# The order of two DFTs turned round, with block products in the second

## The chip, the cores and the metric

The kernel runs on one core of one Trainium2 chip. The metric is the device time of one execution in microseconds. A core has a matrix engine (TensorE, PE in the profile, with its weight loads as PEld), three elementwise engines (VectorE or DVE, ScalarE or ACT, GpSimd or POOL), and SyncE (SP), which here issues the DMAs. Each engine works through its own list of instructions in order; a DMA issued by SP or POOL waits in that list until its buffers are free.

## The reference

```python
x = A_x                                             # 2048 tokens x 448
n = layernorm(x)
a = n @ dft_hid_re.T ; b = n @ dft_hid_im.T         # DFT over the 448 features
h = x + dft_seq_re @ a - dft_seq_im @ b             # DFT over the 2048 tokens, real part
m = layernorm(h)
out = h + (gelu(m @ w_gate) * (m @ w_up)) @ w_down  # 448 -> 1792 -> 448
```
All inputs are float32.

## The kernel before

Every float32 operand of a matmul is kept as two float16 parts, a high half written by ACT (`hi_part`, line 105) and a low half written by DVE (`lo_part`, lines 109 and 111), and a product is three matmuls: high by high, low by high, high by low.

**The DFT stage.** The sequence DFT runs first, on the normalised x. There are four blocks b of 512 output tokens and 16 chunks c of 128 input tokens, so 64 steps n. In a step, `seq_mm` (line 412) holds a 128 x 128 piece of x as the stationary operand and streams 512 columns of W past it; the last 64 features of both parts (re and im) share one bank and are done by `seq_mm_rest` (line 426), two matmuls side by side in the array. Seven PSUM banks collect a block. W arrives as 128 x 1024 float32 tiles (`seq_load`, five buffers), and `seq_hi` and `seq_lo` split it three steps ahead. When a block is done, `z_out` moves the banks to SBUF in two halves, and `hid_mm` (line 477) does the feature DFT: 21 matmuls of 448 columns for each 128 tokens, whose result DVE adds to x (line 485). These follow some steps into the next block, from the table `after`.

Beside this, written out by step number in `early` and `after`: the 14 tiles of gate/up weights (`Weights`: load, sums on DVE, split, store to DRAM), the second layernorm and its operands for the first two quarters of tokens (`ffn_stats` to `ffn_transpose`), the store of h, and the first loads and sums of w_down. PE starts with 56 transposes that have no use but activity (line 99).

**The feed-forward stage.** `GateUp` makes products of blocks (line 716, 256 columns) for 4 quarters of tokens x 14 tiles of features, steps t = 0 to 55. From t = 14, `dn_mm` multiplies by w_down with seven block products in place of eight (line 660, 224 columns). `down_prep(t)` prepares w_down in steps 0 to 14: POOL makes sums of blocks, ACT and DVE split them into `wd`. `gw_load` fetches the stored weight tiles again, two steps ahead, into three buffers.

Of the kernel before, what the change touches and what calls it, by code (L numbers as in the profile page):

```python
# [11 lines left out]
ALU = mybir.AluOpType  # L12
# [20 lines left out]
def kernel(  # L33
# [55 lines left out]
    sign_t = const.tile([P, 1], F32, name="sign_t")  # L89
    G.memset(sign_t[:64], D_SC)  # L90
    G.memset(sign_t[64:], -D_SC)

# [4 lines left out]
    pw = ps_tr.tile([P, 8, P], F16, tag="tr", name="pw")  # L97
    for k in range(56):
        PE.transpose(pw[:, k % 8, :], ident, ident)  # L99
# [61 lines left out]
    def pair_tile(name):  # L161
        return ring.tile([P, 2, D], F32, tag="xh", bufs=5, name=name)

    def w_tile(name):
        return ring.tile([P, 28 * P], F16, tag="w", bufs=3, name=name)
# [125 lines left out]


    class Weights:


        def __init__(self, f):
            self.f = f
            self.raw = dft.tile([P, 2, 6, P], F32, tag="raw", bufs=2, name=f"gu_raw{f}")
            for r in range(2):
                nc.sync.dma_start(self.raw[:, r], w_gu[f, :, r])  # L300

        def sums(self):
            gate, up = self.raw[:, 0], self.raw[:, 1]
            s = self.s = dft.tile([P, 10, P], F32, tag="s", name=f"gu_s{self.f}")
            V.tensor_add(s[:, 0:3], up[:, 0:3], up[:, 3:6])
            V.tensor_sub(s[:, 3:6], s[:, 0:3], gate[:, 0:3])
            V.tensor_sub(s[:, 6:8], gate[:, 0:2], up[:, 0:2])
            V.tensor_sub(s[:, 8:10], gate[:, 4:6], s[:, 4:6])
# [15 lines left out]
        def split(self, of_raw):  # L324
            if of_raw:
                self.w = w_tile(f"gu_w{self.f}")
# [9 lines left out]
    xt, xs, norm_x = {}, {}, {}  # L336

    def x_load(i):
        xt[i] = dft.tile([P, 1, D], F32, tag="xt", bufs=3, name=f"x{i}")
        nc.sync.dma_start(xt[i][:, 0, :], x[i * P : (i + 1) * P, :])  # L340

    def x_stats(i):
        mv = stats(xt[i], f"x{i}")
        norm_x[i] = mv, root(mv, f"x{i}")

    def x_norm(i):
        mv, sd = norm_x.pop(i)
        xn = xt[i][:, 0, :]
        normed(xn, xn, mv, rstd(mv, sd, f"x{i}"), 0)
        xs[i] = dft.tile([P, 2, D], F16, name=f"xs{i}")  # L350
        hi_part(xs[i][:, 0], xn)

    def x_lo(i):
        lo_part(xs[i][:, 1], xt[i][:, 0, :], xs[i][:, 0])

    wr, ws = {}, {}

    def seq_load(n):
        wr[n] = dft.tile([P, 8 * P], F32, tag="wr", bufs=5, name=f"wr{n}")
        b, q, jj = n // NT, n // 2 % 8, n % 2
        nc.sync.dma_start(wr[n], w_seq[(2 * b + jj) * 8 + q])

    def seq_hi(n):
        if n % 2 == 0:
            ws[n // 2] = dft.tile([P, 2, 2, 8 * P], F16, tag="ws", bufs=4, name=f"ws{n // 2}")
        hi_part(ws[n // 2][:, 0, n % 2], wr[n], D_SC)

    def seq_lo(n):
        t = ws[n // 2][:, :, n % 2]
        lo_part(t[:, 1], wr[n], t[:, 0], D_SC)


    def first_load(c, jj):
        if c == 0:
            wr[jj] = dft.tile([P, 8 * P], F32, tag="wr", bufs=5, name=f"wr{jj}")
        if c == jj == 0:
            ws[0] = dft.tile([P, 2, 2, 8 * P], F16, tag="ws", bufs=4, name="ws0")  # L380
        cols = slice(c * P, (c + 1) * P)
        nc.sync.dma_start(wr[jj].rearrange("p (b t) -> p b t", b=4)[:, :, cols], w_seq[jj * 8][:, :, cols])

    def first_views(c, jj):
        cols = slice(c * P, (c + 1) * P)
        ts = [wr[jj], ws[0][:, 0, jj], ws[0][:, 1, jj]]
        return [t.rearrange("p (b t) -> p b t", b=4)[:, :, cols] for t in ts]

    def first_hi(c, jj):
        src, hi, lo = first_views(c, jj)  # L390
        hi_part(hi, src, D_SC)

    def first_lo(c, jj):
        src, hi, lo = first_views(c, jj)
        lo_part(lo, src, hi, D_SC)

    def seq_w(n, l, part):

        t = ws[n // 2][:, l].rearrange("p a (r g c t) -> p r c a g t", r=2, g=2, c=2)
        return t[:, part, n % 2]  # L400

    TERMS = ((0, 0), (1, 0), (0, 1))
    acc = {}

    def seq_mm(n, parts, terms=range(3)):

        b, c = divmod(n, NT)
        for part in parts:
            for k in range(3):
                for m in terms:  # L410
                    lx, lw = TERMS[m]
                    PE.matmul(  # L412
                        acc[b, 3 * part + k],
                        xs[c][:, lx, k * P : (k + 1) * P],
                        seq_w(n, lw, part),
                        start=c == 0 and m == 0,
                        stop=c == NT - 1 and m == 2,
                    )

    def seq_mm_rest(ns):  # L420

        for n in ns:
            b, c = divmod(n, NT)
            for m, (lx, lw) in enumerate(TERMS):
                for part in range(2):
                    PE.matmul(  # L426
                        acc[b, 6][64 * part : 64 * part + 64, :],
                        xs[c][:, lx, 3 * P :],
                        seq_w(n, lw, part),
                        start=c == 0 and m == 0,  # L430
                        stop=c == NT - 1 and m == 2,
                        skip_group_check=True,
                    )

    z = {}

    def z_out(b, k):
        if k == 0:
            z[b] = dft.tile([P, 2, 7, TB], F16, tag="z", name=f"z{b}")
        sc = 1.0 / (X_SC * D_SC)  # L440
        ps = acc.pop((b, k))
        hi_part(z[b][:, 0, k], ps, sc)
        lo_part(z[b][:, 1, k], ps, z[b][:, 0, k], sc)


    wh = dft.tile([P, 2, 7, D], F16, name="wh")
    wh_raw = {}

    def wh_load(g):

        t = wh_raw[g] = dft.tile([P, (3, 3, 1)[g], D], F32, tag="raw", bufs=2, name=f"wh_raw{g}")
        if g < 2:
            nc.sync.dma_start(t, w_hid[:, 0:3, g * D : (g + 1) * D])
        else:
            for r in range(2):
                nc.sync.dma_start(t[64 * r : 64 * r + 64, 0], w_hid[64 * r : 64 * r + 64, 3, r * D : (r + 1) * D])

    def wh_split(g):
        src = wh_raw[g]
        k = slice(3 * g, 3 * g + src.shape[1])  # L460
        sc = (D_SC, -D_SC, sign_t)[g]
        hi_part(wh[:, 0, k], src, sc)
        lo_part(wh[:, 1, k], src, wh[:, 0, k], sc)

    hp = {}
    xr = x.rearrange("(k g j p) d -> k j p g d", k=2, g=2, j=4)

    def h_tile(q, j):
        hp[q, j] = pair_tile(f"hx{q}_{j}")
        nc.sync.dma_start(hp[q, j], xr[q // 2, 2 * (q % 2) + j])  # L470

    def hid_mm(b, i, pool, tag):

        y = pool.tile([P, 512], F32, tag=tag, name=f"y_{b}_{i}")
        for k in range(7):
            for m, (lz, lw) in enumerate(((0, 0), (0, 1), (1, 0))):
                PE.matmul(  # L477
                    y[:, :D],
                    z[b][:, lz, k, i * P : (i + 1) * P],
                    wh[:, lw, k, :],  # L480
                    start=k == 0 and m == 0,
                    stop=k == 6 and m == 2,
                )
        h = hp[b, i // 2][:, i % 2, :]
        V.scalar_tensor_tensor(h, y[:, :D], 1.0 / D_SC, h, op0=ALU.mult, op1=ALU.add)  # L485

    def h_store(q, j):
        nc.sync.dma_start(h_dram[2 * q + j], hp[q, j])


    N_STEPS = NB * NT
    gu = {}

    early, after = {}, {}

    def at(where, n, *what):
        where.setdefault(n, []).extend(what)

    for g in range(3):
        at(early, 5 + 2 * g, lambda g=g: wh_load(g))  # L500
        at(early, 7 + 2 * g, lambda g=g: wh_split(g))

    for k, f in enumerate(reversed(range(NF))):
        n = 17 + 3 * k
        at(early, n - 4, lambda f=f: gu.update({f: Weights(f)}))
        at(early, n, lambda f=f: gu[f].sums())
        at(early, n + 1, lambda f=f: gu[f].split(True))
        at(early, n + 2, lambda f=f: gu[f].split(False), lambda f=f: gu[f].store())
    for b in range(NB):
        for j in range(2):  # L510
            n = (b + 1) * NT + 1 + 6 * j
            at(early, min(n - 4, N_STEPS - 3), lambda b=b, j=j: h_tile(b, j))
            if b == NB - 1:
                continue
# [15 lines left out]
    for c in range(2):  # L530
        for jj in range(2):
            first_load(c, jj)
# [608 lines left out]
```

## Time and profile before

| what | value |
|---|---|
| median of 3 runs | 732.07 us (731.82 to 732.6) |
| profiled execution: first to last instruction | 730.1 us |
| around that span, against the median of the runs | 2.0 us |
| PE busy | 718.5 us (98%) |
| DVE / ACT / POOL busy | 523.0 / 277.9 / 242.1 us |
| moved by DMA | 139.84 MB, mean 192 GB/s |

The profiled execution has no time of its own apart from its span; the 2.0 us are the distance to the median of the other runs. In the profile, a group of instructions is given as line, engine, operation, output<-inputs, shapes and count, then the busy time, the mean time of one in ns, and the idle time of the engine just before them with what ended it. Matmuls overlap in the array, so their pace is read from the chain of work, where one piece begins when the piece before lets it.

### The profile page before, as it was taken

The page shows a single profiled execution, that of the slowest core. Times are in us where ns is not written, and L with a number is a line of the kernel's source. Part 1 is how long each engine was busy: PE and PEld are TensorE (multiplying, and loading weights), DVE is VectorE, ACT ScalarE, POOL GpSimd, SP SyncE. Part 2 cuts the span into 40 slices and gives each one's busy share as a digit, 9 for nine tenths or more (in the row PEclk, how much of TensorE's full clock was granted, in tenths as well). Part 3 has the DMA queues.
Part 4 walks back from the last instruction along what each step waited for, and adds up shares of the span by engine and source line. Part 5 has one row for each costly group of instructions (what it writes and reads, how often), then busy time and mean ns, then how long its engine had stood idle before and what let it go on. Part 6 is the DMA issues. An engine that isn't in the chain of part 4 may idle for free.

```text
span 730.1 us, 13452 instructions
## 1 busy us (share of the span) xinstructions
PE 718.5 (98%) x5309; PEld 497.9 (68%) x5309; DVE 523.0 (72%) x1071; ACT 277.9 (38%) x544; POOL 242.1 (33%) x281
## 2 busy tenths in 40 slices
PE   9999999999999999999999999999999999999987
PEld 5444444444444444444588889999999999999977
DVE  7888667486665866441377778787887877989794
ACT  4444703256233442311043444442444434454421
POOL 0000000000000001000057865576685867768360
PEclk9999999999999999999999999999999999999999
DMA  8667466577667976530057654747447676555311
GB/s 280 227 218 235 163 231 208 185 211 256 231 214 218 316 253 241 219 122 5 26 206 262 240 207 167 181 168 209 176 147 225 186 213 228 219 179 185 127 39 39
DMA packets 63503, 139.84 MB, mean 192 GB/s; under 512 B 30288, under 2 KB 39504, under 8 KB 63440
## 3 DMA queue, kind: packets, MB, share of 16 engines
q1 hardware_dynamic: 63440, 138.99, 57.2%
q8 instruction: 41, 0.67, 0.4%
q14 instruction: 22, 0.18, 0.1%
HBM read 112.23 MB, written 20.19 MB: 181 GB/s over the span
## 4 chain that ended last, share of the span: by engine, by line
PE 93%; DVE 4%; DMA 1%; ACT 1%; issue 1%; POOL 0%; POOLq 0%; DVEq 0%; ACTq 0%
PE acc L412 34%; PE pY L716 13%; PE acc_d L660 12%; PE y L477 9%; PE pZ L716 9%; PE pX L716 9%; PE acc L426 6%; DMA gw<-w_dram 1%; PE pw L99 1%; DVE last_v L900 1%; DVE last_a L109 1%; DVE last_s L904 1%; PE last_Y L879 1%; PE last_X L879 1%; DVE last_s L903 0%
## 5 line engine op out<-in xcount | busy, mean ns | idle before, releaser
L412 PE MATMUL acc<-ws,xs 128*128 128x512 f16 x1152 | 253.8, 379 | 0.0
L716 PEld LDWEIGHTS <-gw 128*128 128x128 f16 x2067 | 201.9, 98 | 24.1 <-issue 2.4
L412 PEld LDWEIGHTS <-xs 128*128 128x128 f16 x1152 | 111.3, 98 | 138.3 <-issue 6.5
L716 PE MATMUL pY<-hops,gw 128*128 128x256 f16 x901 | 123.0, 273 | 1.9 <-DVE u L726 1.7
L660 PE MATMUL acc_d<-wd,dn_w 128*128 128x224 f16 x882 | 105.1, 259 | 0.0
L203 POOL TENSOR_TENSOR wd_s<-wd 128x448 f32<-128x448 f32 x7 | 7.9, 1131 | 273.8 <-DVE gu_w L111 273.8
L111 DVE SCALAR_TENSOR_TENSOR ws<-wr,ws 128x1024 f16<-128x1024 f32 (+1 forms) x66 | 78.0, 1188 | 15.5 <-ACT ws L105 15.2
L105 ACT ACTIVATE ws<-wr 128x1024 f16<-128x1024 f32 (+1 forms) x66 | 66.3, 1021 | 57.3 <-DMA wr<-in_w_seq_dram 28.1
L660 PEld LDWEIGHTS <-dn_w 128*128 128x128 f16 x882 | 85.0, 98 | 2.9
L716 PE MATMUL pX<-hops,gw 128*128 128x256 f16 x583 | 81.0, 273 | 0.8 <-DMA gw<-w_dram 0.8
L716 PE MATMUL pZ<-hops,gw 128*128 128x256 f16 x583 | 79.2, 273 | 0.0
L783 POOL TENSOR_TENSOR hh<-hh,g 128x256 f32<-128x256 f32 x42 | 31.0, 738 | 143.9 <-DVE hh L726 142.8
L726 DVE SCALAR_TENSOR_TENSOR u<-pY,u 128x256 f32<-128x256 f32 x112 | 46.9, 419 | 27.4 <-ACT c L790 18.8
L485 DVE SCALAR_TENSOR_TENSOR hx<-y,hx 128x448 f32<-128x448 f32 x16 | 10.0, 625 | 77.8 <-PE y L477 77.8
L477 PE MATMUL y<-wh,z 128*128 128x448 f16 x336 | 65.7, 352 | 0.0
L754 ACT ACTIVATE u<-pX 128x256 f32<-128x256 f32 x56 | 21.4, 383 | 90.3 <-PE pX L716 90.2
L477 PEld LDWEIGHTS <-z 128*128 128x128 f16 x336 | 32.8, 98 | 31.6 <-issue 0.4
L109 DVE TENSOR_TENSOR dn_w<-dn_s,dn_w 128x640 f16<-128x640 f32 x42 | 53.0, 1261 | 1.6 <-ACT dn_w L105 1.2
L767 ACT ACTIVATE g<-pX 128x256 f32<-128x256 f32 x56 | 21.5, 384 | 74.3 <-PE pX L716 69.0
L792 POOL TENSOR_TENSOR hh<-hh,c 128x256 f32<-128x256 f32 x42 | 41.2, 981 | 17.2 <-ACT c L790 17.0
L426 PE MATMUL acc<-ws,xs 128*64 128x512 f16 x384 | 44.7, 381 | 0.0
L810 POOL TENSOR_TENSOR dn_s<-hh 128x256 f32<-128x256 f32 x42 | 43.4, 1034 | 0.0
(112 smaller groups left out, 829.4 us busy)
## 6 DMA issues: line engine op xcount, KB each, us to landing
gw<-w_dram SPq DMA_DIRECT2D x53, 896.0 KB, 4.8
wr<-in_w_seq_dram SPq DMA_DIRECT2D x62, 512.0 KB, 5.9
w_dram<-gu_w SPq DMA_DIRECT2D x14, 896.0 KB, 4.7
gu_raw<-in_w_gu_dram SPq DMA_DIRECT2D x28, 384.0 KB, 5.6
wd<-in_w_down_dram SPq DMA_DIRECT2D x14, 448.0 KB, 5.6
x<-in_x_dram SPq DMA_DIRECT2D x16, 224.0 KB, 2.8
hx<-in_x_dram SPq DMA_DIRECT2D x8, 448.0 KB, 6.7
h_dram<-hx SPq DMA_DIRECT2D x8, 448.0 KB, 2.7
```

Source lines behind the costliest of these rows:

```text
L105: A.activation(dst, src, AF.Copy, scale=scale)
L109: V.tensor_sub(dst, src, hi)
L111: V.scalar_tensor_tensor(dst, src, scale, hi, op0=ALU.mult, op1=ALU.subtract)
L412: PE.matmul(acc[b, 3 * part + k], xs[c][:, lx, k * P : (k + 1) * P], seq_w(n, lw, part), start=c == 0 and m == 0, stop=c == NT - 1 and m == 2,
L426: PE.matmul(acc[b, 6][64 * part : 64 * part + 64, :], xs[c][:, lx, 3 * P :], seq_w(n, lw, part), start=c == 0 and m == 0, stop=c == NT - 1 ...
L477: PE.matmul(y[:, :D], z[b][:, lz, k, i * P : (i + 1) * P], wh[:, lw, k, :], start=k == 0 and m == 0, stop=k == 6 and m == 2,)
L660: PE.matmul(acc[k // 2][:, k % 2 * HD : (k % 2 + 1) * HD], a_of(la, a), b_of(lb, b), start=first and m == 0 and k % 2 == 0, stop=last and ...
L716: PE.matmul(ps, w[:, wl, wa + ws, :], ops[:, m + ms, :], start=first and n == 0, stop=last and n == len(terms) - 1, skip_group_check=True,)
L726: V.scalar_tensor_tensor(dst, ps, SC, other, op0=ALU.mult, op1=ALU.add)
L783: G.tensor_mul(c21, c21, self.g1)
L792: G.tensor_mul(c22, c22, self.c12)
L810: G.tensor_sub(s[:, 2:4], t[:, 1:4:2], t[:, 0:4:2])
```

## The change

The feature DFT runs first. Tiles of x are normalised, split, and transposed (the first four tiles by PE through PSUM and ACT, the others by DMA), and `feature_mm` makes a and b for 16 tiles of 128 tokens, 22 matmuls of 448 columns each. `feature_out` keeps them in SBUF in two halves. The sequence DFT then holds a 128 x 128 piece of W as the stationary operand and streams 448 columns of a or b.

It runs in 8 passes p of 256 output tokens, and a pass in 8 units u of two chunks. Six units of a pass are plain: 24 matmuls of 448 columns. Two (u = 6, 7, four of the 16 chunks) use seven products of blocks with 224 columns in place of eight, 42 matmuls. The sums of W that these need are made in transfers: SP fills seven slots from DRAM, four of them with the same block, and POOL issues DMAs that add further blocks to them, in three steps that wait for one another. The sums of a and b are made by POOL (`feature_sums`). `seq_out` puts four banks of a pass together and adds x.

Pass 0 is mixed with the feature DFT in the order of `slots`: two tiles, then one unit. `plan(n, rank, what)` puts side work into slot n, lower ranks first, ahead of slot n's matmuls. The 14 weight tiles are spread over slots 25 to 75 of 80. In the feed-forward stage `down_prep` runs three steps later; w_down's first loads come at the end of the DFT stage; the last statistics come in steps 23 to 25; the activation table for gelu is loaded ahead; and the third weight buffer has its own pool, so that the first reload takes the place of tile 0's weights.

The diff, cut to its core:

```diff
-    ps_tr = ctx.enter_context(tc.tile_pool(name="ps_tr", bufs=1, space=bass.MemoryType.PSUM))
-    ps_seq = right.enter_context(tc.tile_pool(name="ps_seq", bufs=7, space=bass.MemoryType.PSUM))
+    ps_dft = right.enter_context(tc.tile_pool(name="ps_dft", bufs=4, space=bass.MemoryType.PSUM))
-    for k in range(56):
+    for k in range(50):
         PE.transpose(pw[:, k % 8, :], ident, ident)
...
+    N_PASS, N_UNIT = 8, 8
+    S_UNITS, WR = (6, 7), 3
+    ORDER = (0, 1, 2, 6, 3, 7, 4, 5)
...
+    def x_turn_pe(i, k0, k1):
...
+        for k in range(k0, k1):
+            PE.transpose(ptr[i][:, k, :], xs[i][:, k * P : (k + 1) * P], ident)
+        A.activation(xT[i][:, k0:k1, :], ptr[i][:, k0:k1, :], AF.Copy)
...
+    def seq_load(p, u):
+        w = w_seq[p * N_UNIT + u]
+        if not is_s(u):
+            t = wr[p, u] = dft.tile([P, 4, 2 * P], F32, tag="wr", bufs=WR, name=f"wr{p}_{u}")
+            for g in range(2):
+                nc.sync.dma_start(t[:, 2 - 2 * g : 4 - 2 * g, :], w[:, g::2, :])
+            return
+        t = wr[p, u] = dft.tile([P, 7, 2 * P], F32, tag="wr7", bufs=2, name=f"wr{p}_{u}")
+        nc.sync.dma_start(t[:, 3:7, :], w[:, 1:2, :].to_broadcast([P, 4, 2 * P]))
+        nc.sync.dma_start(t[:, 0, :], w[:, 3, :])
+        nc.sync.dma_start(t[:, 1:3, :], w[:, 0:3:2, :])
+
+    def seq_add(p, u, step):
+        w, t = w_seq[p * N_UNIT + u], wr[p, u]
+        def add(s0, s1, k):
+            n = s1 - s0
+            G.dma_start(t[:, s0:s1, :], w[:, k : k + 1, :].to_broadcast([P, n, 2 * P]), accum_op=ALU.add)
+        if step == 0:
+            add(3, 4, 0)
+            add(4, 7, 3)
+        else:
+            add(4 + step, 7, (0, 2)[step - 1])
+
+    def seq_split(p, u):
+        r = wr.pop((p, u))
+        t = ws[p, u] = dft.tile([P, 2, 7, 2 * P], F16, tag="ws", bufs=3, name=f"ws{p}_{u}")
+        n = 7 if is_s(u) else 4
+        hi_part(t[:, 0, :n], r, D_SC)
+        lo_part(t[:, 1, :n], r, t[:, 0, :n], D_SC)
...
+            if is_s(u):
+                for a, o, k, half in PRODUCTS:
+                    for m, (lb, lw) in enumerate(TERMS):
+                        mm(k, slice(half * HD, half * HD + HD), w[:, lw, a, cc * P : (cc + 1) * P], b[:, lb, o], end and m == 2)
+            else:
+                for k, a0 in ((0, 2), (1, 0)):
+                    for r in range(2):
+                        for m, (lb, lw) in enumerate(TERMS):
+                            rhs = b[:, lb, 2 * r : 2 * r + 2].rearrange("p o d -> p (o d)")
+                            mm(k, slice(0, D), w[:, lw, a0 + r, cc * P : (cc + 1) * P], rhs, end and r == 1 and m == 2)
+
+    def seq_out(p):
+        X, Y, Z, W = acc.pop(p)[0]
+        h = hp[divmod(p, 2)]
+        e = fops.tile([P, 4, HD], F32, tag="tt", name=f"e{p}")
+        stt = V.scalar_tensor_tensor
+        A.activation(e[:, 1], Z[:, 0:HD], AF.Copy, scale=SC_Y)
+        stt(h[:, 0], X[:, 0:D], SC_Y, h[:, 0], op0=ALU.mult, op1=ALU.add)
+        stt(e[:, 0], W[:, 0:HD], -SC_Y, e[:, 1], op0=ALU.mult, op1=ALU.add)
+        stt(h[:, 1], Y[:, 0:D], SC_Y, h[:, 1], op0=ALU.mult, op1=ALU.add)
+        stt(e[:, 3], W[:, HD:D], SC_Y, e[:, 0], op0=ALU.mult, op1=ALU.subtract)
+        stt(e[:, 0], Z[:, HD:D], -SC_Y, e[:, 0], op0=ALU.mult, op1=ALU.add)
+        stt(e[:, 2], Z[:, HD:D], SC_Y, e[:, 3], op0=ALU.mult, op1=ALU.add)
+        for g in range(2):
+            G.tensor_add(h[:, g], h[:, g], e[:, 2 * g : 2 * g + 2].rearrange("p o d -> p (o d)"))
...
+        plan(n - 2, 3, lambda p=p, u=u: seq_split(p, u))
+        if is_s(u):
+            plan(n - 9, 9, lambda p=p, u=u: seq_load(p, u))
             for k in range(3):
+                plan(n - 6 + k, 9, lambda p=p, u=u, k=k: seq_add(p, u, k))
         else:
+            plan(max(n - WR - 2, 0) if p == 0 else n - WR - 2, 9, lambda p=p, u=u: seq_load(p, u))
...
     def gw_load(t):
-        gw[t] = w_tile(f"gw{t}")
+        gw[t] = w_tile(f"gw{t}", ring if t % 3 < 2 else ring3)
...
+    for g in range(2):
+        at(side, (23 + g, 1), lambda g=g: ffn_moments(NB - 1, 1, hp[NB - 1, 1], g))
+    at(side, (25, 4), lambda: ffn_rstd(NB - 1, 1))
...
-        if t <= 2 * NC:
-            down_prep(t)
...
+            if t == 2:
+                down_sums(0)
+            if t > 2:
+                down_prep(t - 3)
...
+        if t - 3 <= 2 * NC:
+            down_prep(t - 3)
```

More of the change, by code (lines that the diff above doesn't have):

```diff
@@ new lines, in x_stats, with x_rstd @@
+    def x_stats(*tiles):
+        n, tag = len(tiles), f"x{tiles[0]}"
+        mv = small.tile([P, n, 2], F32, tag=f"mv{n}", name=f"mv_{tag}")
+        for g, i in enumerate(tiles):
+            st = small.tile([P, 6], F32, tag="st", name=f"st_x{i}")
+            V.bn_stats(st, xt[i][0])
+            V.bn_aggr(mv[:, g, :], st)
+        norm_x[tiles] = mv, root(mv, tag)
+    def x_rstd(*tiles):
+        mv, sd = norm_x.pop(tiles)
+        r = rstd(mv, sd, f"x{tiles[0]}")
+        for g, i in enumerate(tiles):
+            norm_x[i] = mv, r, g
@@ new lines, with feature_mm @@
+    feat = {}
+    def feature_mm(i, parts=range(2), tag="B"):
+        if 0 in parts:
+            feat[i] = [ps_dft.tile([P, 512], F32, tag=tag, name=f"ab{i}_{r}") for r in range(2)]
+        steps = [[], [(k, wh_lo, k) for k in range(4)]]
+        for k in range(4):
+            steps[0] += [(k, wh_hi, k)] + ([(4 + k, wh_hi, k)] if k < 3 else [])
+        for part in parts:
+            for n, (kx, w, kw) in enumerate(steps[part]):
+                for r in range(2):
+                    PE.matmul(
+                        feat[i][r][:, :D],
+                        xT[i][:, kx, :],
+                        w[:, kw, r * D : (r + 1) * D],
+                        start=part == 0 and n == 0,
+                        stop=part == 1 and n == 3,
+                    )
@@ L420, in seq_mm_rest @@
[L420 to L433, printed above, removed]
@@ L458, in wh_split @@
[L458 to L485, printed above, removed]
@@ L487, in h_store @@
[L487 to L508, printed above, removed]
@@ new lines @@
+    plain = [u for u in ORDER if not is_s(u)]
+    late = [("U", 0, v) for v in sorted(ready, key=lambda v: ORDER.index(v))]
+    early = [("U", 1, u) for u in plain[:1]]
+    slots += early + late
+    mixed = plain[:]
+    for n, s in enumerate(S_UNITS):
+        mixed.insert(1 + n * 8 // len(S_UNITS), s)
+    for p in range(1, N_PASS):
+        slots += [("U", p, u) for u in mixed if ("U", p, u) not in early]
+    where = {s: n for n, s in enumerate(slots)}
+    units = [s[1:] for s in slots if s[0] == "U"]
@@ new lines @@
+    order = list(reversed(range(2, NF))) + [0, 1]
+    at_f = [n0 + k * (len(slots) - 3 - n0) // NF for k in range(NF)]
+    plan(n0 - 3, 9, lambda: gu.update({order[0]: Weights(order[0])}))
+    for k, f in enumerate(order):
+        n = at_f[k]
+        plan(n, 7, lambda f=f: gu[f].sums())
+        plan(n + 1, 7, lambda f=f: gu[f].split(True))
+        if k + 1 < NF:
+            plan(n + 1, 9, lambda f=order[k + 1]: gu.update({f: Weights(f)}))
+        plan(n + 2, 7, lambda f=f: gu[f].split(False), lambda f=f: gu[f].store())
@@ new lines @@
+    x_turn_pe(1, 0, 4)
+    x_turn_pe(1, 4, 7)
+    x_rstd(2, 3)
+    x_bias(2, 3)
+    x_norm(2)
+    x_lo(2)
+    feature_mm(1, (0,))
+    x_turn_pe(2, 0, 4)
+    x_turn_pe(2, 4, 7)
+    for k in range(3):
+        wh_low(k)
+    x_norm(3)
+    x_lo(3)
+    feature_mm(2, (0,), "A")
+    feature_mm(0, (1,))
+    feature_out(0)
+    feature_mm(1, (1,))
+    x_turn_pe(3, 0, 4)
+    x_turn_pe(3, 4, 7)
+    feature_out(1)
+    feature_mm(2, (1,))
+    p2 = ring3 = None
+    for n in range(min(todo), len(slots)):
+        for _, what in sorted(todo.pop(n, ()), key=lambda t: t[0]):
@@ L589 @@
[L589 to L600 removed]
+            continue
+        kind, *k = slots[n]
@@ L603 @@
+        if kind == "F":
+            feature_mm(*k)
+        else:
+            p, u = k
+            mine = [s[2] for s in slots if s[0] == "U" and s[1] == p]
+            seq_mm(p, u, u == mine[0], u == mine[-1])
+    for n in sorted(todo):
+        for _, what in sorted(todo.pop(n), key=lambda t: t[0]):
+            what()
+    seq_out(N_PASS - 1)
+    h_store(N_PASS - 1)
+    down_load(0)
+    down_load(1)
+    gw = {f: gu[f].w for f in range(3)}
+    right.close()
     right.close()
```

373 lines of the change are left out of this document (205 added, 168 removed).

## The prediction

> **What bounds the kernel now.** I read the totals of the page first, then the stretches, then the chain that ended last.
>
> ```profile
> span 730.1 us, 13452 instructions
> ...
> PE 718.5 (98%) x5309; PEld 497.9 (68%) x5309; DVE 523.0 (72%) x1071; ACT 277.9 (38%) x544; POOL 242.1 (33%) x281
> ...
> PE 93%; DVE 4%; DMA 1%; ACT 1%; issue 1%; POOL 0%; POOLq 0%; DVEq 0%; ACTq 0%
> ```
> TensorE (PE) has 11.6 us without work in 730.1 and is 93% of the chain. The stretches (us, busy time of PE, weight loads, DVE, ACT, POOL, granted clock, DMA share, GB/s) say where:
>
> ```profile
> 7.10:364.90 357.80, 357.76 (x1875) 164.41 (x1873) 228.32 (x480) 128.31 (x204) 2.84 (x3) 1.00 0.61 203
> 364.90:425.00 60.10, 57.59 (x524) 51.03 (x523) 44.47 (x90) 27.06 (x57) 42.41 (x45) 1.00 0.65 231
> 434.00:697.00 263.00, 263.00 (x2524) 244.91 (x2522) 215.62 (x433) 109.36 (x261) 178.13 (x205) 1.00 0.57 185
> 245.00:255.00 10.00, 10.00 (x48) 4.56 (x47) 6.90 (x12) 4.16 (x6) 0.00 (x0) 1.00 1.01 328
> ```
> The DFT stage is 7.10 to 364.90. PE never waits in it, so it is worth what its matmuls are worth. DVE is busy 64% of it, the DMA engines 61% at 203 GB/s, hence about 333 GB/s when full; the last row, full for 10 us at 328, agrees.
>
> What a matmul costs when they run back to back is read from the chain (start, us, piece), not from the mean of a group, since one matmul's own 260 to 380 ns overlap the next:
>
> ```profile
> 60.05 2.71 PE acc L426 x24
> 62.76 15.65 PE acc L412 x72
> ...
> 87.05 3.97 PE y L477 x21
> ...
> 438.28 0.96 PE acc_d L660 x10
> ...
> 444.55 0.96 PE acc_d L660 x10
> ```
> 512 columns cost 15.65/72 = 217 ns, the paired 64-wide ones 2.71/24 = 113, 448 columns 3.97/21 = 189, 224 columns 96. The group row below divides to 119 for the last (105.1/882), but that counts tails twice: the step between the two L660 pieces is 6.27 us, and 42 such steps are the 263.00 us of the stretch, so 96 holds.
>
> **The matmuls.**
>
> ```profile
> L412 PE MATMUL acc<-ws,xs 128*128 128x512 f16 x1152 | 253.8, 379 | 0.0
> L660 PE MATMUL acc_d<-wd,dn_w 128*128 128x224 f16 x882 | 105.1, 259 | 0.0
> L477 PE MATMUL y<-wh,z 128*128 128x448 f16 x336 | 65.7, 352 | 0.0
> L426 PE MATMUL acc<-ws,xs 128*64 128x512 f16 x384 | 44.7, 381 | 0.0
> ```
> Removed: 1152 x 0.2174 + 384 x 0.1129 + 336 x 0.189 = 250.4 + 43.4 + 63.5 = 357.3 us, which is the stretch. Added: the feature DFT, 16 tiles x 22 matmuls of 448 columns; in each of 8 passes six plain units of 24 matmuls of 448 and two block units of 42 of 224. That is (352 + 1152) x 0.189 + 672 x 0.096 = 284.3 + 64.5 = 348.8 us. The difference is **-8.5 us**. Nearly all is the block products: a plain unit costs 4.54 us and a block unit 4.03, and 16 x 0.51 = 8.1.
>
> **The start.** Before, a tile is used as it lies; after, it must be split in both halves, transposed and copied out of PSUM before the first matmul.
>
> ```profile
> 1.37 5.89 PE L99 MATMUL pw<-ident 128*128 128x128 f16 x56 [1.37 <-POOL sign_t L90]
> ...
> 3.22 0.63 DVE L119 BATCH_NORM_STATS2 st_x<-x 128x6 f32<-128x448 f32 x1 [3.22 <-DMA x<-in_x_dram]
> ...
> 5.21 0.51 DVE L142 TENSOR_SCALAR x<-x,mv_x,r_x 128x448 f32<-128x448 f32 x1
> ...
> 6.04 0.56 ACT L105 ACTIVATE xs<-x 128x448 f16<-128x448 f32 x1
> 6.63 0.62 DVE L109 TENSOR_TENSOR xs<-x,xs 128x448 f16<-128x448 f32 x1 [0.31 <-ACT xs L105]
> ...
> 7.10 7.07 PE L412 MATMUL acc<-ws,xs 128*128 128x512 f16 x32
> ```
> ```profile
> L105 ACT ACTIVATE wh<-wh_raw 128x1344 f16<-128x1344 f32 x2 | 2.6, 1308 | 0.0
> ```
> By these rows tile 0's low half is ready at about 7.3; ACT copies four transposes out by 7.8, then owes a quarter of w_hid (896 elements, 0.9 us by the row of 1344) before the other three, 9.2. It owes two more quarters and tile 1's high half until 11.7, so the first 14 matmuls end near 12.0. Tile 1's copies end at 13.4, its 14 matmuls at 16.1; tile 2's copies at 17.0, its matmuls at 19.7; the second parts of three tiles (24 matmuls) and tile 3's transposes, at 24.7. PE has done 66 x 0.189 = 12.5 us of the counted matmuls since 7.1, so **+5 us** are lost. Below, the 28 transposes alone (55 ns each by the pace of L660) are +1.5; above, I take twice my working, +10. I keep the middle, since each of its steps has a row.
>
> Those 56 warm-up transposes ran at 5.89/56 = 105 ns, while 128 columns at the later pace would take 55: the array starts at half pace. [...]
>
> **DVE and ACT beside PE.**
>
> ```profile
> L111 DVE SCALAR_TENSOR_TENSOR ws<-wr,ws 128x1024 f16<-128x1024 f32 x62 | 75.3, 1221 | 15.5 <-ACT ws L105 15.2 <-DMA wr<-in_w_seq_dram 0.3
> L111 DVE SCALAR_TENSOR_TENSOR z<-acc,z 128x512 f16<-128x512 f32 x28 | 18.2, 690 | 28.2 <-ACT z L105 28.2
> L623 DVE SCALAR_TENSOR_TENSOR hr<-acc_d,hr 128x224 f32<-128x224 f32 x28 | 10.2, 384 | 2.6 <-PE acc_d L660 2.3
> L485 DVE SCALAR_TENSOR_TENSOR hx<-y,hx 128x448 f32<-128x448 f32 x16 | 10.0, 625 | 77.8 <-PE y L477 77.8
> ```
> The split of W grows from 78 us to 48 x 1.22 + 16 x 2.14 (1792 elements) = 92.8; z (18.2) and L485 go; the features' low halves cost 24 x 0.625 + 4 x 2.1 = 23.4; seq_out costs 8 x (2 x 0.625 + 4 x 0.384) = 22.3; the norms moved to ACT give back some 11. DVE comes to about 250 of 353 us, 71%. It is densest in passes 1 to 4:
>
> ```profile
> L111 DVE SCALAR_TENSOR_TENSOR gu_w<-gu_s,gu_w 128x512 f16<-128x512 f32 x28 | 18.0, 685 | 0.0
> L306 DVE TENSOR_TENSOR gu_s<-gu_s,gu_raw 128x384 f32<-128x384 f32 x14 | 7.8, 558 | 0.5
> L180 DVE BATCH_NORM_STATS2 st_h<-hx 128x6 f32<-128x448 f32 x16 | 9.8, 613 | 0.1
> L109 DVE TENSOR_TENSOR xs<-tt,xs 128x768 f16<-128x768 f32 x8 | 8.4, 1054 | 0.0
> ```
> There a pass has 11.6 us of W splits, 2.8 of seq_out, 2.2 weight tiles of 4.4 (two sums like L306 and two smaller ones, 3.5 lows like L111), 2.4 of statistics and some 4.9 of operands, together 31.4 against 35.3 of PE. A split is queued two units (9 us) ahead of its matmuls. So **0**, with +3 as its bound if POOL's adds in seq_out hold it up. POOL had 2.84 us of work in the whole stage.
>
> **The transfers.** Columns: KB of one, median us to landing.
>
> ```profile
> wr<-in_w_seq_dram SPq DMA_DIRECT2D x62, 512.0 KB, 5.9
> w_dram<-gu_w SPq DMA_DIRECT2D x14, 896.0 KB, 4.7
> gu_raw<-in_w_gu_dram SPq DMA_DIRECT2D x28, 384.0 KB, 5.6
> hops<-xs SPq DMA_TRANSPOSE x32, 5.8
> ```
> A block unit fills seven slots of 131 KB and adds seven more instead of filling four: 16 x 10 x 0.131 = 21 MB more, and the x transposes 2.7 MB. With 203 GB/s x 357.8 us = 72.6 MB before, that makes some 96 MB in 353 us, 272 GB/s, 82% of 333. So the stage as a whole fits. It is tighter in passes 1 to 4: W 6 x 0.524 + 2 x 14 x 0.131 = 6.8 MB, 2.2 weight tiles of 1.70 MB = 3.75, h 0.9, operand transposes 0.8, in all 12.3 MB, 36.9 us at 333 GB/s against 6 x 4.54 + 2 x 4.03 = 35.3 us of PE. Four passes fall behind by 4 x 1.6 = 6.4 us. A W load is issued three units before its split (13 us) and lands in 5.9, so 7 us of lead absorb it. I charge **+1 us**.
>
> No accumulating DMA is in the trace. [...] I take the plain price because the nearest row is the plain load of the same bytes. The chain of three adds has 24 us from the landing to the split, 8 us each, so latency alone does not decide. POOL issues these 64 DMAs; two waits for earlier adds can stand ahead of seq_out's adds there, and behind those h's statistics on DVE.
>
> **After the DFT.**
>
> ```profile
> 381.80 0.83 PE L716 MATMUL pX<-hops,gw 128*128 128x256 f16 x6 [0.80 <-DMA gw<-w_dram]
> L111 DVE SCALAR_TENSOR_TENSOR wd<-wd_s,wd 128x1120 f16<-128x1120 f32 x7 | 11.1, 1582 | 0.0
> L767 ACT ACT_TABLE_LOAD x1 | 1.3, 1283 | 0.0
> ```
> The gate/up products need no seq_out, and their banks are those of pass 6 first, so PE goes on. The first weight reload now replaces the buffer of tile 0, not of tile 2: the 0.80 us wait goes, **-0.8**. w_down's preparation moves three steps later, into steps with down products, where DVE is 82% busy (215.62/263): two pieces of 1.58 and one of 0.76 meet four steps with 1.1 us of slack each; 0, at most +2.5. The late Sqrt costs ACT (42% busy) two table loads of 1.28; 0 to +1.5.
>
> Sum: -8.5 + 5 + 1 - 0.8 = -3.3 us, span 726.8. The median of the runs, 732.07, is 2.0 over the span of 730.1; I keep that distance: **728.8 us**.
>
> **Rivals.** First, *the adding DMAs fill the rings* (slower). If an add takes as long as 1.5 plain loads, a pass carries 13.2 MB, 39.7 us against 35.3; four passes fall 17 behind, 7 are absorbed, +10, that is 738 to 739; at double, 42.4 us, +21, 749. It decides once a pass needs more than 35.3 us and a quarter of the lead, 37 us or 12.3 MB, so the plain price is at the edge. For it: the row at share 1.01 shows that these engines do fill. Against it: most of the stage has room.
>
> [...]
>
> Second, *the start costs twice my working*: PE's stops let the array fall back to the half pace of the first 7 us, and the 12.5 us of matmuls there take up to 5 more: 733.8. For it: PE would stand still for most of 7 to 12 us. Against it: transposes and matmuls are scattered in it.
>
> Third, *w_down late*: DVE overloaded in steps 14 to 17, +2.5: 731.3, no change. For it: the stretch 364.9 to 425 already has 2.5 us without matmuls.
>
> **The numbers.** My forecast 0.50, the rings 0.28, the start 0.14, w_down 0.08. The forecast's own range is 723 (start +1.5, other waits of the last stage gone too, no stall) to 730.6. The range to 741 takes in the second and third rival and the milder half of the first; the double price, under 2 in 10 with what lies below 723, is left out. A difference under 0.2% (1.5 us) can't be told from none here. Faster 0.52 (the forecast, a little of the third), same 0.08, slower 0.40.
>
> **What would show it.** The pace of the block products at 96 ns and plain ones at 189; the first feature matmul near 8, slot 3 begun near 25 us; the DFT's last matmul near 361; DMA share about 0.8 in passes 1 to 4 and no PE idle ended by DMA; no wait on gw at the first reload. Wrong it is if PE in passes 1 to 4 waits for splits that wait for W, most of all for the adds.

## The result, and the profile after

The changed kernel takes **814.31 us** (median of 4 runs, 810.1 to 818.75) where the kernel before takes 731.98 (731.82 to 732.6): ratio 1.1121, 95% interval 1.108 to 1.1161. It is 82 us slower. The forecast was 728.8, its range 723 to 741. The profiled execution took 818.75 us, 1.85 over its span.

These lines of the page of the kernel after answer to the totals and the chain of before; the last two are its DMA queues (packets, MB, share of 16 engines' span).

```profile
span 816.9 us, 14587 instructions
...
PE 738.3 (90%) x5635; PEld 554.5 (68%) x5635; DVE 555.7 (68%) x1071; ACT 317.1 (39%) x585; POOL 354.1 (43%) x374
...
q1 hardware_dynamic: 104256, 148.27, 59.4%
q0 software_dynamic: 15360, 14.68, 11.8%
...
PE 48%; DMA 22%; DVE 12%; issue 7%; ACT 5%; POOL 4%; SPq 2%; ACTq 0%; DVEq 0%; POOLq 0%
```

PE went from 93% of the chain to 48%, and DMA from 1% to 22%. The stretches of the kernel after (same columns as before) say where:

```profile
0.00:24.00 24.00, 18.43 (x124) 11.71 (x125) 13.61 (x37) 12.97 (x22) 5.96 (x10) 1.00 0.58 197
24.00:113.00 89.00, 81.02 (x448) 42.86 (x446) 49.77 (x114) 44.07 (x73) 24.76 (x22) 1.00 0.68 144
113.00:445.00 332.00, 279.92 (x1683) 170.50 (x1684) 195.55 (x334) 110.69 (x155) 80.53 (x68) 0.93 0.93 240
445.00:817.00 372.00, 358.91 (x3384) 329.43 (x3381) 296.79 (x588) 149.38 (x337) 242.89 (x274) 0.99 0.55 179
```

The DFT now ends at 445 us instead of 364.9. That is 80 us, nearly the whole loss. From 24 to 445 us PE is idle for 8.0 + 52.1 = 60 us, and by an estimate its mean clock of 0.93 in the third row is worth another 332 x 0.07 = 23 us. The feed-forward takes 372 us instead of 365.2, the other 7 us. Neither DVE nor ACT nor POOL is near full in the third row, so the waits are the next view (total, times, longest; us):

```profile
POOL wr L472 <- DMA wr<-in_w_seq_dram: 160.0, 27, 10.2
DVE ws L106 <- ACT ws L100: 138.0, 23, 13.0
ACT ws L100 <- DMA wr<-in_w_seq_dram: 118.6, 20, 13.2
...
PE acc L502 <- ACT ws L100: 34.4, 10, 8.5
...
PE acc L502 <- DVE ws L106: 22.8, 17, 1.8
```

`wr` is W as loaded, `ws` its split halves, and L472 issues the adds. POOL waits for one add before it issues the next. ACT waits for a block unit's last add before it makes the high half. DVE waits for ACT. PE waits for both halves of the split: 34.4 + 22.8 = 57 of its 60 idle us. One block unit, in the timeline of the kernel after (start, us, engine, line):

```profile
222.40 0.70 SPq L463 DMA_DIRECT2D wr<-in_w_seq_dram  x1
...
234.54 3.10 POOL L472 DMA_DIRECT2D wr<-in_w_seq_dram  x3 [4.92 <-DMA wr<-in_w_seq_dram]
...
247.81 1.23 POOL L472 DMA_DIRECT2D wr<-in_w_seq_dram  x1 [10.18 <-DMA wr<-in_w_seq_dram]
...
255.46 3.10 POOL L472 DMA_DIRECT2D wr<-in_w_seq_dram  x3 [6.42 <-DMA wr<-in_w_seq_dram]
...
262.03 1.70 ACT L100 ACTIVATE ws<-wr 128x1792 f16<-128x1792 f32 x1 [8.07 <-DMA wr<-in_w_seq_dram]
...
263.76 2.03 DVE L106 SCALAR_TENSOR_TENSOR ws<-wr,ws 128x1792 f16<-128x1792 f32 x1 [6.80 <-ACT ws L100]
```

The load is issued at 222.40 and the split begins at 262.03, 40 us later. The plan gives it seven units, n−9 to n−2, some 31 us at the full pace of 4.4 us a unit. The first adds go out 12 us after the load, in a group with the last add of the block unit before (x3): POOL's list is in order, and that add stood ahead. From there three rounds take 27.5 us, 9.2 us each. While ACT and DVE stand at this unit's split (idle for 8.07 and 6.80 us), the plain units behind it are not split either: ACT begins none between 252.91 and 266.25. The load could not have gone much earlier: there are two buffers for block units, and in the same timeline the split of two block units before ended on DVE at 221.30, 1.1 us ahead of this load. More lead therefore needs a third buffer.

### The profile page after: what moved, and what is told of

Its sections match the earlier page's. It is cut to its first block, busy times and chain, and to the rows that moved or that the text cites. A ratio compares the mean times of both kernels' runs of the same rounds, so it can differ in the third digit from the quotient of the medians.

```text
span 816.9 us, 14587 instructions
## 1 busy us (share of the span) xinstructions
PE 738.3 (90%) x5635; PEld 554.5 (68%) x5635; DVE 555.7 (68%) x1071; ACT 317.1 (39%) x585; POOL 354.1 (43%) x374
## 3 DMA queue, kind: packets, MB, share of 16 engines
q0 software_dynamic: 15360, 14.68, 11.8%
## 4 chain that ended last, share of the span: by engine, by line
PE 48%; DMA 22%; DVE 12%; issue 7%; ACT 5%; POOL 4%; SPq 2%; ACTq 0%; DVEq 0%; POOLq 0%
DMA wr<-in_w_seq_dram 17%; PE pY L859 11%; PE acc_d L802 10%; PE acc L502 10%; PE pX L859 7%; PE pZ L859 7%; ACT ws L100 2%; DVE ws L106 2%; PE ab L404 2%; DMA gu_raw<-in_w_gu_dram 2%; DVE gu_w L106 2%; DMA gw<-w_dram 2%; DMA x<-in_x_dram 1%; POOL wr L472 1%; DVE dn_w L104 1%
## 5 line engine op out<-in xcount | busy, mean ns | idle before, releaser
L502 PE MATMUL acc<-b,ws 128*128 128x448 f16 (+1 forms) x1824 | 304.0, 331 | 57.5 <-ACT ws L100 34.4
L502 PEld LDWEIGHTS <-ws 128*128 128x128 f16 x1824 | 183.8, 103 | 177.3 <-ACT ws L100 39.3
L106 DVE SCALAR_TENSOR_TENSOR ws<-wr,ws 128x1024 f16<-128x1024 f32 x64 | 97.1, 1522 | 138.2 <-ACT ws L100 138.0
L472 POOL DMA_DIRECT2D wr<-in_w_seq_dram x64 | 68.8, 1226 | 191.8 <-DMA wr<-in_w_seq_dram 160.0
L100 ACT ACTIVATE ws<-wr 128x1024 f16<-128x1024 f32 x64 | 76.8, 1210 | 168.3 <-DMA wr<-in_w_seq_dram 118.6
L926 POOL TENSOR_TENSOR hh<-hh,g 128x256 f32<-128x256 f32 x42 | 35.6, 847 | 58.5 <-DVE hh L869 56.6
L536 POOL TENSOR_TENSOR hx<-hx,e 128x448 f32<-128x448 f32 x16 | 25.1, 1584 | 81.9 <-DVE e L533 31.7
L404 PEld LDWEIGHTS <-xT 128*128 128x128 f16 x352 | 33.9, 98 | 35.6 <-ACT xT L370 2.2
L404 PE MATMUL ab<-wh_hi,xT 128*128 128x448 f16 x224 | 45.9, 353 | 2.8 <-DMA xT<-xs 1.3
L952 POOL TENSOR_TENSOR dn_s<-hh 128x256 f32<-128x256 f32 x42 | 43.3, 1031 | 0.0
L953 POOL TENSOR_TENSOR dn_s<-hh 128x256 f32<-128x256 f32 x42 | 42.7, 1017 | 0.0
```

Source lines behind the costliest of these rows:

```text
L100: A.activation(dst, src, AF.Copy, scale=scale)
L106: V.scalar_tensor_tensor(dst, src, scale, hi, op0=ALU.mult, op1=ALU.subtract)
L404: PE.matmul(feat[i][r][:, :D], xT[i][:, kx, :], w[:, kw, r * D : (r + 1) * D], start=part == 0 and n == 0, stop=part == 1 and n == 3,)
L472: G.dma_start(t[:, s0:s1, :], w[:, k : k + 1, :].to_broadcast([P, n, 2 * P]), accum_op=ALU.add)
L502: PE.matmul(banks[k][:, cols], lhs, rhs, start=k not in begun, stop=stop, skip_group_check=True)
L952: G.tensor_add(s[:, 0:2], t[:, 0:2], t[:, 2:4])
```

## The experiments

Where an experiment leaves out part of the computation, its expectation says so. Single times (e1, e2, e3, e7, e8, e9) are one run each; the kernel before had a median of 732.2 to 732.6 beside all of them.

**Which part of the adds costs.** Three edits, each alone: no add waits for another of its unit (e1), the same transfers without the accumulation (e2), and 13 of 14 raw gate/up loads left out (e3).

```
e1  -            add(4 + step, 7, (0, 2)[step - 1])
    +            d = scr[next(scr_n) % 4][:, : 3 - step, :]
    +            G.dma_start(d, w[...same source...], accum_op=ALU.add)
e2  -            G.dma_start(t[:, s0:s1, :], w[...], accum_op=ALU.add)
    +            G.dma_start(t[:, s0:s1, :], w[...])
e3  +            if gu:
    +                self.raw = next(iter(gu.values())).raw
    +                return
```

> The second and third adds of a block unit go to scratch tiles instead of on top of the first, so that no add waits for another; slots 5 and 6 lack these terms. Same transfers, same bytes, same issuing engine. Theory A (chain: POOL issues in order, so block units come no faster than one landing of the first add plus one of the second, about 12 + 7.6 = 20 us in the changed kernel's trace, against 17.6 us of matmuls): the DFT stage falls to within some 10 us of its matmuls, time near 745. Theory B (rings full: the DMA share of 0.93 from 113 to 445 us is the bound, adds at twice the price of a plain load): nothing moves by more than 10 us, time 800 to 815.

> The POOL transfers overwrite their slots instead of adding to them; same order, same waits, same bytes. By the queue rows an added KB takes about 0.10 us of an engine and a plain one 0.05. Theory B: 14336 KB x 0.05 / 16 = 45 us of ring time go, time 765 to 775. Theory A: the three landings shorten from 9.9, 7.6 and 6.4 to 6 to 7 each, the period to 13, under the 17.6 of matmuls: time 740 to 750.

> All 14 gate/up weight tiles are made from the first tile's raw load; 13 x 0.79 MB are not loaded, the rest stands. Theory B: 13 x 2.1 us of ring time go, time 785 to 792. Theory A: landings shorten a little under the lighter load, 795 to 810. A third theory (SP's list: loads of W stand behind the raw load, which waits for DVE): its 47 us of waits on SP go, time under 780.

Measured: 783.98 (−30), 789.8 (−24.5) and 802.72 (−11.6). Each gives back a part and none the whole. e1 and e2 lie outside the ranges of both of their theories, e3 in the range of its theory A. The queue line of e2's page against after's and before's gives the price of an add:

```profile
q0 software_dynamic: 4608, 14.68, 7.2%
```
```profile
q1 hardware_dynamic: 63440, 138.99, 57.2%
```

The first is e2, span 788.0; the second is the kernel before. An add costs 0.118 x 16 x 816.9 / 14.68 = 105 us of one engine per MB. The same bytes copied on the same queue cost 62, and before's queue as a whole 48. So an add costs 1.7 such copies and 2.2 times what before's queue costs per byte. How much of that is the adding itself is not settled: the copies went in 4608 packets, the adds in 15360.

**e4: the same products, the sums made by POOL.** Four blocks are loaded as they are, and POOL adds them in SBUF; no adding DMA is left.

```
-        t = wr[p, u] = dft.tile([P, 7, 2 * P], ...)
-        nc.sync.dma_start(t[:, 3:7, :], w[:, 1:2, :].to_broadcast([P, 4, 2 * P]))
+        t = wr[p, u] = dft.tile([P, 8, 2 * P], ...)
+        nc.sync.dma_start(t[:, 7, :], w[:, 1, :])
...
-            add(3, 4, 0)
-            add(4, 7, 3)
+            G.tensor_add(t[:, 3], t[:, 7], t[:, 1])
+            G.tensor_add(t[:, 4], t[:, 7], t[:, 0])
-            add(4 + step, 7, (0, 2)[step - 1])
+            G.tensor_add(t[:, 4 + step], t[:, 3 + step], t[:, step])
```

> The sums of W of the block units are made by POOL from four loaded blocks (four adds of 128x256 float32, about 0.75 to 1.0 us each), no adding DMAs, no repeated loads; all results as the reference's. Both theories: DFT stage within 10 us of its matmuls, time 727 to 740. If it stays above 760, the loss is in something else of the new order (SP's list, DVE). Against the kernel before: my sum of the prediction with 7.5 us lost at the start, as the changed trace shows, gives 730 plus what the feed-forward stage lost, 731 to 737.

Measured: **737.87**, ratio 1.0078 (1.0061 to 1.0095). Stretches of e4:

```profile
113.00:364.00 251.00, 250.24 (x1613) 156.31 (x1612) 205.88 (x326) 106.77 (x150) 87.00 (x63) 1.00 0.78 238
...
425.00:455.00 30.00, 25.95 (x229) 22.92 (x228) 25.08 (x46) 13.65 (x29) 23.33 (x25) 0.94 0.46 159
```

The DFT's stalls are gone: 0.8 us of idle PE in 251, ended at 364. So 76 of the 82 us belong to the sums made by transfers: the adding DMAs and the three slots of each unit that were loaded again for them. A new place shows in the second row: around 425 to 455 us PE loses 4 us while DVE and POOL are 84% and 78% busy. Its timeline there:

```profile
430.36 1.49 DVE L106 SCALAR_TENSOR_TENSOR wd<-wd_s,wd 128x1120 f16<-128x1120 f32 x1
...
432.47 0.74 ACT L100 ACTIVATE dn_w<-dn_s 128x640 f16<-128x640 f32 x1 [1.27 <-POOL dn_s L948]
...
434.45 0.71 PE L854 MATMUL pY<-hops,gw 128*128 128x256 f16 x5 [2.29 <-DVE u L864]
```

A piece of w_down (`wd`) stands in DVE's list, POOL's sums for the down products (`dn_s`) are late for ACT, and the small `u` that PE needs comes 2.29 us late behind them.

**e5 and e6: two versions built on e4 too early.** e5 finishes w_down's preparation by step 13, by putting two pieces into some steps. e6 adds a third block unit per pass.

```
e5  +    PREP = {t: [] for t in range(NF)}
    +    for k in range(2 * NC):
    +        PREP[3 + k * 11 // (2 * NC)].append(k)
    -                down_prep(t - 3)
    +            for k in PREP[t]:
    +                down_prep(k)
e6  as e5, and S_UNITS = (5, 6, 7)
```

> POOL makes the sums of W as in the run before with POOL sums, and w_down's preparation ends at feed-forward step 13 (14 pieces over steps 3 to 13) instead of running to step 17 beside the first down products; all results as the reference's. If the 4 us of idle PE in 425 to 455 us there and the half clock after it come from that preparation, they go: 731 to 733, no difference from the kernel before. If they come from something else (the shifted loads, statistics in steps 23 to 25), 736 to 738 as before the edit.

> The same with three block units in a pass instead of two. 8 x 0.51 = 4.1 us of matmuls less: 727 to 729 if DVE (0.9 us more for each such unit) and POOL keep up; 733 or more if DVE, already 82% busy from 113 to 364 us with two, becomes the bound.

Measured: 741.05 (ratio 1.012, 1.0101 to 1.0139), outside both of its ranges, and 789.15 (1.0784, 1.0769 to 1.0798), which its rival allowed, though not for the reason given: DVE is 73% busy from 113 to 410 us. In e5 the stall only moved ahead, into steps 12 to 14; the stretch of e5 where e4 had 13.48 us of PE in 15:

```profile
415.00:430.00 15.00, 9.61 (x75) 7.79 (x74) 9.81 (x18) 5.47 (x11) 11.76 (x11) 0.88 0.36 126
```

In e6 the block loads, planned nine units ahead with two buffers, stood in SP's list for a buffer, and what was queued behind them waited (ACT 65.4 us for loads of W). Its waits of SP's queue:

```profile
SPq L463 <- DVE ws L106: 143.1, 17, 17.8
```

**e7: e1 and e2 together.**

> The changed kernel with both edits at once: the second and third transfers of a block unit go to scratch tiles, and all overwrite instead of adding. What is left against the run with POOL sums is the price of the bytes alone (21 MB more through rings and SP's list). If the two losses add up (30 for the waits between adds, 24 for their price), 757 to 763; if both act through the same full rings, 770 to 780; if the bytes alone cost nothing, 738 to 745.

Measured: 765.49 (−49). That is between the ranges, in none of them: the two parts come near to adding up (30 + 24.5 = 54.5), and 28 us over e4 stay.

**e8 and e9: period or lateness.** e8 has one block unit per pass, so units come twice as far apart. e9 is e8 with more lead and no other difference.

```
e8  -    S_UNITS, WR = (6, 7), 3
    +    S_UNITS, WR = (6,), 3
e9  as e8, and
    -            plan(n - 9, 9, lambda p=p, u=u: seq_load(p, u))
    +            plan(max(n - 13, 0) if p == 0 else n - 13, 9, ...)
    -                plan(n - 6 + k, 9, ...seq_add(p, u, k))
    +                plan(n - 10 + 2 * k, 9, ...seq_add(p, u, k))
```

> The changed kernel with one block unit in a pass, sums still by adding DMAs. Block units then come every 35 us, so that one landing after the other (about 20 to 25 us by the changed kernel's trace) fits between them, and the rings lose 8 x 10 slots: by the chain and by the rings alike nearly all of the loss goes but the 4.1 us of matmuls, 740 to 748. If one unit costs half of what two cost, 775 to 780, the price is paid per unit, by its own latency, and not by either queue.

> One block chunk of 16 rows per pass (as in e8, 789.15), but the block unit's load is planned thirteen units ahead instead of nine, and its three rounds of adds ten, eight and six units ahead instead of six, five and four; bytes, packets and number of adds are the same as in e8. Theory A (the chain of adds comes too late for its split, and the split blocks ACT's and DVE's lists): with four more units (18 us) of lead the split finds its sums there, ACT's waits for W loads and adds fall below 20 us, and the time is 740 to 755. Rival B (what costs is the adds' occupation of the DMA rings and the loads queued behind them, whenever they are issued): the time stays at 780 to 790. In between, each would have a part.

e8: 789.15, over both of its ranges; with units twice as far apart 57 us over before stay, so their rate alone was not the limit. e9: **751.05**. The rows are stretches of e8, then of e9, each from 113 us to near the DFT's end:

```profile
113.00:417.00 304.00, 272.86 (x1529) 152.55 (x1528) 186.94 (x331) 105.07 (x154) 49.91 (x40) 0.96 0.80 226
```
```profile
113.00:378.00 265.00, 259.56 (x1512) 146.05 (x1511) 180.41 (x328) 104.01 (x150) 42.87 (x36) 1.00 0.91 256
```

Same packets, same bytes, 38 us less: lateness alone was worth that. PE's idle time fell from 31 to 5 us and its clock rose to 1.00. ACT still waited 74.7 us for W in e9 (92.1 in e8), more than the 20 expected, but PE was idle for only 5 of the 265 us.

**e10 and e11: w_down where it was, and three block units again.**

```
e10 +    plan(len(slots) - 6, 9, lambda: down_load(0))
    +    plan(len(slots) - 2, 9, lambda: down_sums(0))
    ...
    +        if t <= 2 * NC:
    +            down_prep(t)
    -                down_prep(t - 3)
e11 as e10, S_UNITS = (5, 6, 7), block loads at n - 6, sums at n - 4 + k // 2
```

(The tags of `wd32` change places, so that the first chunk's buffer is free before the last seq_out.)

> e4 (sums of W by POOL, no adding DMA; 737.87) with w_down's preparation put back to where it was in the kernel before: the first chunk's load and sums in pass 7, pieces in steps 0 to 13 of the feed-forward instead of 3 to 16. Theory (the 6 to 7 us that e4's feed-forward takes longer come from w_down's pieces that stand in DVE's and POOL's lists in steps 14 to 16, ahead of the small operations that PE waits for): the feed-forward returns to 361 to 364 us and the time to 731 to 734. Rival (they come from h's last statistics, the table loads or the reloads of gate/up weights, all unchanged here): 737 to 739.

> As e10, with three block units of eight per pass instead of two (eight more block units at 4.03 instead of 4.54 us: -4.1), their loads planned six units ahead instead of nine and POOL's sums three to four units ahead, so that no load stands in SP's list waiting for one of the two block buffers. Theory (e6's 789 was SP held up by early loads that waited for a buffer): SP's waits for split tiles of W vanish and the time is e10's less 2 to 4, 727 to 732. Rival (three block units a pass are too much for the DMA rings, ACT and DVE): stalls stay in passes 1 to 4, 745 or more.

e10: **733.74**, ratio 1.002 (1.001 to 1.0031). The same place of the feed-forward, in e10:

```profile
430.00:455.00 25.00, 24.85 (x239) 22.98 (x237) 19.38 (x42) 10.85 (x25) 15.11 (x17) 1.00 0.48 167
```

No stall and no fall of the clock: w_down's pieces in steps 14 to 16 were worth 4.1 us in the median. e10's feed-forward takes 366.9 us, a little over the 361 to 364 expected. Its DFT ends at 365.0 us, where before's ended at 364.9, so the gain of the products is used up even without a stall. e11: 758.02 (1.0365, 1.0329 to 1.04), in its rival's range. Its waits show where it loses: the sums, now two units behind the load, come too late for the split. Whether the plan or the load on rings and engines makes them late is not shown.

```profile
ACT ws L100 <- POOL wr L473: 98.0, 17, 9.2
```

**e12, e13, e14: the change with more lead.** e12 is the change with e9's plan and a third block buffer (`tag="wr7", bufs=3`). e13 adds e10's w_down. e14 is e11 with three block buffers of seven slots, loads at n−9, and two plain buffers instead of three.

> The change as it is, with a third buffer for block units' W, their loads planned thirteen units ahead instead of nine, and the three rounds of adds ten, eight and six units ahead instead of six, five and four. Bytes, packets and adds are unchanged. Theory A (lateness of the adds is the loss): PE's stalls in 113 to 445 us go nearly all, the DFT ends at 365 to 375 and the time is 737 to 750, close to e4's 737.87. Rival B (the rings are full: adds at double price make a pass of 35.3 us of PE carry more than the rings take, as the first rival of the prediction had it): the stalls come back as W loads that land late, 765 to 800.

> e12 with w_down's preparation in the place of the kernel before, as in e10. Theory A: e12 less 4, and not under e10's 733.7, as the start and the products are the same: 734 to 746. Rival B: as e12, 760 to 795.

> As e11 (three block units a pass, sums by POOL, w_down early), but with three block buffers of seven slots instead of two of eight, two plain buffers instead of three to make room, block loads nine units ahead again and POOL's sums six to four units ahead. If e11's loss (758.0) was that block loads and sums came late, this gives e10's 733.7 less up to 4, 730 to 736. If three block units a pass are too much for ACT, DVE and the rings in any case, or two plain buffers now make the plain loads late, 745 or more.

e12: **771.28**, ratio 1.0537 (1.0502 to 1.0572). e13: **766.23**, 1.0464 (1.045 to 1.0479). Both lie in the ranges of rival B, and yet 43.0 of the 82 us went, so lateness had a part too. e12 changes lead and buffers together, and their shares were not separated; e9 had shown the lead alone, for one unit per pass. What is left shows in the stretches of e13 against e10:

```profile
113.00:290.00 177.00, 163.31 (x1026) 98.41 (x1024) 129.61 (x224) 73.76 (x104) 54.12 (x46) 0.99 1.10 275
```
```profile
113.00:254.00 141.00, 140.64 (x909) 87.95 (x908) 121.10 (x206) 67.06 (x96) 50.22 (x37) 1.00 0.82 242
```

In e13 the DMA engines are full (share 1.10, and 275 GB/s where before's full stretch moved 328). In e10 they are at 0.82. An estimate from the rows: per pass the adds cost 14 x 0.131 MB x 105/16 = 12.0 us of all engines and the six extra loaded slots (three for each of two units) 2.4. With e10's 0.82 x 35.3 = 28.9 that is 43.3 us at share 1, or 39.4 at the 1.10 reached, against 35.3 us of PE. Seven passes with 4.1 us each make 29; measured between e10 and e13: 32.5.

e14: 770.46 (1.052, 1.0506 to 1.0535), in the second of its ranges. ACT waited 96.5 us for W loads there; that the missing plain buffer did this is likely, but no run shows it alone. Whether three block units could pay with room for all buffers stays open; no version here beat the kernel before.

## Why the prediction was wrong, point by point

Between the changed kernel and before, the runs make a ladder: more lead with a third buffer −43.0 (e12), w_down early −5.1 (e13), sums by POOL instead of adding DMAs and repeated loads −32.5 (e10), and 1.5 are left. e10 is 5 us over the forecast: by its trace 2.6 at the end of the DFT (365.0 against 364.9 − 8.5 + 5 + 1 = 362.4), about what the start was under-priced by, and 2.5 in the feed-forward. The split between the first and the third depends on this order: without adding DMAs the plan's old lead is enough (e4).

**The matmuls (−8.5): right.** In e10's chain, where nothing stalls, a block unit and a plain unit cost what was worked out:

```profile
79.14 4.03 PE acc L497 x42
91.48 4.54 PE acc L497 x24
```

**The transfers (+1): the step that failed.** Two sentences of it were wrong. "I take the plain price because the nearest row is the plain load of the same bytes": an add costs 2.2 times what a byte of before's queue costs (105 against 48 us of one engine per MB). "8 us each, so latency alone does not decide": a round took 9.2 us, the first waited behind the add of the unit before in POOL's list, and the split came some 9 us behind its plan. The working took this for one unit's affair. But the split stands in the in-order lists of ACT and DVE ahead of the plain units' splits, so its lateness reaches PE through those too, at every block unit (e8 to e9: 38 us for 8 of them, 4.8 each). The stalls also lowered PE's clock, the 23 us above, for which the sum has no term. The closing sentence of the prediction named this as what would make it wrong; it got no price.

**DVE and ACT (0): right as far as shown.** In e4 and e10, which have no adding DMA, DVE is 82% and 83% busy from 113 us to the DFT's end, and PE is idle for less than 1 us.

**The first rival (rings, 0.28): right in kind, and too small.** Its double price gave +21 us; e13 against e10 gives +32.5. It had charged four passes, but the load on the engines lasts to the DFT's end; the later stretch of e10:

```profile
219.00:364.00 145.00, 145.00 (x934) 90.52 (x932) 117.23 (x172) 58.01 (x79) 56.54 (x39) 1.00 0.79 246
```

The trace of before shows no add: the plain price was that of another transfer, and the double one, with its 749, was the author's assumption. The measured 1.7 and 2.2 lie on both sides of double. Choosing the plain price was wrong, but the double price alone would not have given 814 either: with more lead and w_down early the kernel takes 766 (e13).

**The start (+5): about +8, inside its bounds.** PE's timeline of the kernel after:

```profile
19.81 2.44 PE L404 MATMUL ab<-wh_hi,xT 128*128 128x448 f16 x12 [0.21 <-ACT xT L370]
22.09 3.19 PE L404 MATMUL ab<-wh_lo,xT 128*128 128x448 f16 x16
...
27.87 2.43 PE L404 MATMUL ab<-wh_hi,xT 128*128 128x448 f16 x12
```

Tile 2's first products end near 22.2 instead of 19.7, and tile 3's begin at 27.9 instead of 24.7. The 12 matmuls from 19.81 to 22.09 take 190 ns each, the full pace (189), so it is the working, not the second rival's half clock, that was 3 us short. (The clock column could not decide this: it shows 1.00 from 0 to 24 us, although the 50 warm-up transposes there took 5.51 us, 110 ns each against the 55 estimated from 96 ns for 224 columns.)

**After the DFT (−0.8) and w_down (0): wrong by 7.** The wait on gw stayed, 1.1 us in the kernel after (0.36 at the first reload, 0.71 at a later one; before, 0.80 at the first):

```profile
L859 PE MATMUL pX<-hops,gw 128*128 128x256 f16 x583 | 81.6, 274 | 1.1 <-DMA gw<-w_dram 1.1
```

The third rival (w_down, +2.5) was the larger part, at 1.6 times its price: 4.1 us (e4 to e10). Its own working had put 1.58 and 0.76 us of DVE against a slack of 1.1 us a step; POOL's sums of w_down, in the same steps ahead of the down products' sums, were left out of it.

## What to carry to other kernels

Work that came after its turn in one engine's in-order list made all that was queued behind it pay (38 us between e8 and e9): price a late operand by what stands behind its consumer, not by its own latency. The chain of dependent DMAs needed its lead counted in loaded landings (6 to 10 us each here) plus whatever stands ahead in the issuing engine's list; adding that lead, and the buffer that it needs, gave back 43 of 82 us without moving one byte less. And where an engine had room, as POOL in this stage (80.53 of 332 us busy), adding in SBUF was cheaper than adding in the DMA: with 64 adds in SBUF PE was idle for 0.8 of 251 us (e4), and as transfers, with the blocks loaded again for them, they cost 32 us even with the longer lead (e13 to e10).

## What the runs showed of the hardware

An accumulating transfer occupied the engines 2.2 times as long per byte as before's queue as a whole (105 against 48 us of one engine per MB) and 1.7 times as long as the same transfer without accumulation (62); that one went in 4608 packets instead of 15360, and no run separates packet size from adding. Under load one landed in 6.4 us (128 KB) to 9.9 (384 KB), in the rows of issues of the kernel after:

```profile
wr<-in_w_seq_dram POOLq DMA_DIRECT2D x16, 384.0 KB, 9.9
wr<-in_w_seq_dram POOLq DMA_DIRECT2D x32, 128.0 KB, 6.4
```

The granted clock of the kernel after fell from 1.00 (281.6 to 285.1 us) to 0.50 in the DFT; in the stretches of before it is 1.00 throughout. The two stretches that follow:

```profile
285.10:292.00 6.90, 0.33 (x2) 0.00 (x0) 0.00 (x0) 1.71 (x2) 1.75 (x2) 0.91 1.12 309
292.00:295.50 3.50, 1.96 (x10) 1.28 (x11) 3.45 (x5) 1.65 (x3) 0.36 (x1) 0.50 0.63 131
```

PE has nothing to do for 6.6 us, and in the next 3.5 us the clock is 0.50. How long a pause it takes is not shown. So a stall here cost more than its length: over the DFT the lower clock was worth about 23 us, by the estimate above, beside 60 us of idle time.
